# Attention on one core: in half of the row tiles GpSimd adds the row maximum and one exponential serves two tiles

## The chip, the cores and the metric

The kernel runs on one core of one Trainium2 chip. The metric is device time in microseconds (us), the median of several runs. A core has five engines with a queue each, and every queue is worked off in the order of the program: PE (TensorE, matrix products), DVE (VectorE), ACT (ScalarE), POOL (GpSimd) and SP (SyncE, which here only issues transfers). They wait for one another through semaphores. On-chip memory is SBUF (working data) and PSUM (where PE writes its results).

## What is computed

An adaptive layer norm block: attention against a given cache of keys and values, and then a mixer and an MLP. Cut to what matters here:

```python
h = _layernorm(x) * (1 + ca) + sa                       # x: 2048 rows of 640
q = (h @ wq).reshape(B, Sq, H, Dh).transpose(0, 2, 1, 3)   # 32 heads of 128
scores = einsum('bhqd,bhkd->bhqk', q, k_cache) * Dh ** -0.5   # 2048 x 2048 a head
p = softmax(scores, axis=-1)
o = einsum('bhqk,bhkd->bhqd', p, v_cache)
x = x + ga * (o.reshape(B, Sq, H * Dh) @ wo)
# then: layer norm, a shifted mixer with w1 and w2, an MLP with w3 and w4
```

Inputs and the output are bfloat16.

## The kernel before

Attention is cut into 512 *tiles* of 128 query rows against all 2048 keys: 32 heads of 16 tiles each. The loop of line 552 takes one *step* `s` for each tile (`j = s % 16` within the head), and each step appends instructions to the five queues. What a tile goes through:

1. PE: scores into `Sps` in two halves of 1024 columns (`qk`, lines 15 and 301). `Sps` holds one tile, so a half is computed anew only when DVE has read it.
2. DVE: for each half one instruction (line 594) that multiplies the scores by -1/sqrt(128), writes them as float32 into `negS` and keeps the minimum of each row (`nm0`, `nm1`). The minimum of the negated scores is minus the row's maximum. `negS` has three slots; tile `s` uses slot `s % 3`, and DVE may write it when the last reader of tile `s - 3` has finished.
3. POOL: the smaller of the two minima (line 604, `nm`).
4. ACT: the exponential (line 607), which reads `negS` with scale -1 and `nm` as its bias, and writes bfloat16 probabilities into `Pb`, a ring of ten slots (`RP`).
5. The probabilities are transposed into `PTs`, another ring of ten. For most tiles SP issues a transfer that transposes (line 231), for two tiles at once where both of a pair go that way. A few tiles (`PE_STEPS`) are transposed by PE instead, in two halves (line 262), into one of two PSUM banks (`JB`), from where ACT (line 271) or DVE (line 273) copies each half to `PTs`. `by_dve` says which halves DVE takes.
6. PE: the product with V (`pv`, line 314), `PVD` steps after the scores. V has a column of ones, so the row sums come with it.
7. ACT copies the result of two tiles to `Of` (line 585); POOL takes the reciprocal of the sums for four tiles at once (line 455), multiplies (line 462) and issues a transfer to a scratch buffer in HBM for each four tiles (line 469), `LAG` steps later.

Between these, PE computes the Q projection of the next head in pieces (line 246). It uses the same two banks as the transposes, in turn, and ACT casts each finished block of 512 rows (line 253). So PE's next user of a bank waits for the copy out of it.

Heads are of two kinds: those with `h % 4 == 1` (kind 1, eight of them) and the others (kind 0). In kind 0, PE transposes tile 3 in steps 6 and 7 and tile 10 in steps 13 and 14. In kind 1 it transposes tile 2 in steps 5 and 6, tile 3 in 7 and 8, tile 10 in 14 and 15. The pieces of Q fill the other half steps in order, so that casts come in steps 2, 4, 10 and 12 of kind 0, and in 2, 4, 11 and 13 of kind 1.

The order within a step is written out by hand. ACT gets first the copy to `Of` (every second step), then the evacuations and casts of the step, then the exponential. DVE gets the two halves and then its evacuation. POOL gets the minimum, then the reciprocal, the multiplication and the transfer, where there are any. `Prog` (line 20) keeps for each buffer key its last writer and its readers since, and from these puts a semaphore wait in front of an instruction.

After attention the output projection (line 540) and the rest follow in the same program. The first product of the output projection begins while the last tiles are still under way.

## Time and profile before

| | us |
|---|---|
| median of three runs | 1575.56 |
| the three runs | 1574.34, 1575.56, 1580.4 |
| span of the profiled execution | 1568.9 |
| PE busy in it | 1472.3 |
| DVE busy | 1398.3 |
| ACT busy | 1275.9 |
| POOL busy | 623.0 |
| first score tile on DVE starts | 35.4 |
| last exponential ends | 1255.5 |

The profiled execution's own device time is not among the three runs. The profile gives its span, from the first to the last instruction, and the median of the runs lies 6.7 us above it, which is what lies around the span.

How to read it: a line of the groups names the source line, the engine, the operation, the output and input buffers with their shapes and the number of instructions; then the busy time in us, the mean ns of one, and after the second bar the idle time of the engine just before them with what ended it. A line of the timeline begins with the start in us and the duration in us, and in square brackets there is the idle time ahead of it and what released it. An engine's shown durations overlap where one instruction starts before the one in front has quite finished; then the distance from start to start is what an instruction occupies. The granted clock is PE's, as a share of full speed.

### The profile page before, as it was taken

How to read it: one execution, taken by the hardware profiler on the slowest of the kernel's cores; microseconds unless marked ns; L12 is line 12 of the kernel's file. 1: busy time of each engine (PE TensorE's matmuls, PEld its weight loads, DVE VectorE, ACT ScalarE, POOL GpSimd, SP SyncE). 2: the span in 40 equal slices, each digit the busy share in tenths (PEclk: the TensorE clock that was granted, in tenths of full speed). 3: DMA queues.
4: the chain of work that ended last, by engine and by line, in shares of the span. 5: the costliest groups of instructions: out<-in, count | busy, mean ns of one | idle time of the engine just before them, and what ended most of it. 6: DMA issues, size and time to landing. Idle time of an engine off the chain costs nothing.

```text
span 1568.9 us, 33553 instructions
## 1 busy us (share of the span) xinstructions
PE 1472.3 (94%) x13947; PEld 923.4 (59%) x13175; DVE 1398.3 (89%) x2471; ACT 1275.9 (81%) x1121; POOL 623.0 (40%) x1396
## 2 busy tenths in 40 slices
PE   5899999999999999999999999999999899999999
PEld 3466666666665566566656666566566655554545
DVE  6999999999999999999999999999999937667435
ACT  4999999999999999999999999999999900034230
POOL 0144444444444444444444444444444433323100
PEclk9999999999999999999999999999999999999999
DMA  9999999999999999999999999999999999725100
GB/s 298 239 221 239 237 242 237 233 241 243 237 240 233 239 232 232 240 236 235 229 237 236 233 243 249 226 242 243 235 241 237 238 246 190 157 53 144 38 22 34
DMA packets 1172828, 334.59 MB, mean 213 GB/s; under 512 B 1153280, under 2 KB 1166656, under 8 KB 1172672
## 3 DMA queue, kind: packets, MB, share of 16 engines
q1 hardware_dynamic: 1164192, 311.30, 100.8%
q0 software_dynamic: 6144, 16.79, 3.5%
q10 hardware_dynamic: 2336, 4.34, 0.8%
q8 instruction: 108, 1.77, 0.5%
q14 instruction: 48, 0.39, 0.1%
HBM read 43.48 MB, written 19.40 MB: 40 GB/s over the span
## 4 chain that ended last, share of the span: by engine, by line
ACT 40%; DVE 23%; PE 19%; DMA 9%; issue 7%; POOL 1%; POOLq 0%; DVEq 0%
ACT ring L607 32%; DVE negS L594 20%; DMA ring<-ring 8%; PE Sps L540 8%; PE Sps L847 4%; ACT ring L271 3%; ACT kv L253 2%; ACT Of L585 2%; PE QPp L798 2%; PE Oaug L798 2%; DVE ring L273 1%; PE Sps L783 1%; DVE ring L379 1%; DMA negS<-o_scratch 1%; PE PTp L314 1%
## 5 line engine op out<-in xcount | busy, mean ns | idle before, releaser
L594 DVE TENSOR_SCALAR_CACHE_REDUCE negS<-Sps 128x1024 f32<-128x1024 f32 x1024 | 1177.7, 1224 | 19.4 <-PE Sps L15 18.5
L607 ACT ACTIVATE ring<-negS,small 128x2048 bf16<-128x2048 f32 x512 | 1045.7, 2066 | 13.7 <-POOL small L604 12.5
L314 PEld LDWEIGHTS PTp<-kv,ring 128*128 128x128 bf16 x8192 | 554.1, 98 | 325.0 <-issue 69.6
L314 PE MATMUL PTp<-kv,ring 128*128 128x129 bf16 x8192 | 645.3, 220 | 25.0 <-DMA ring<-ring 23.9
L15 PE MATMUL Sps<-kv 128*128 128x512 bf16 x1024 | 387.9, 379 | 16.8 <-DVE negS L594 9.9
L604 POOL TENSOR_SCALAR small<-small 128x1 f32<-128x1 f32 x512 | 146.4, 286 | 621.8 <-DVE negS L594 621.7
L301 PE MATMUL Sps<-kv 128*128 128x512 bf16 x919 | 354.3, 386 | 27.8 <-DVE negS L594 16.5
L462 POOL TENSOR_SCALAR On<-Of,small 128x128 bf16<-128x128 f32 x512 | 191.0, 373 | 13.0
L301 PEld LDWEIGHTS Sps<-kv 128*128 128x128 bf16 x1024 | 98.1, 96 | 141.7 <-DVE negS L594 121.6
L455 POOL TENSOR_TENSOR small<-Of,small 128x4 f32<-128x4 f32 x128 | 133.1, 1040 | 8.8 <-ACT Of L585 8.7
L469 POOL DMA_DIRECT2D o_scratch<-On x128 | 103.1, 806 | 40.8 <-POOL On L462 37.2
L585 ACT COPY Of<-PTp 128x259 f32<-128x259 f32 x256 | 108.6, 424 | 13.2 <-PE PTp L314 13.2
L246 PE MATMUL Oaug<-hTx,kv 128*128 128x512 bf16 x268 | 101.9, 385 | 3.7 <-DVE hTx L411 3.7
L246 PE MATMUL QPp<-hTx,kv 128*128 128x512 bf16 x259 | 97.7, 382 | 2.6 <-ACT hTx L406 2.1
L728 ACT ACT_TABLE_LOAD x1 | 1.3, 1283 | 112.6 <-POOL hTx L746 112.6
L594 DVE DVE_READ_ACCUMULATOR negS<-Sps 128x1 f32 x1024 | 90.3, 88 | 0.0
L271 ACT COPY ring<-Oaug 128x1024 bf16<-128x1024 bf16 x72 | 77.0, 1069 | 0.0
L641 POOL TENSOR_SCALAR negS<-negS 128x1 f32<-128x1 f32 x48 | 24.2, 504 | 125.2 <-DVE negS L650 125.2
L540 PE MATMUL Sps<-wo,negS 128*128 128x128 bf16 (+1 forms) x503 | 69.9, 298 | 1.2 <-DMA negS<-o_scratch 0.8
L540 PE MATMUL Sps<-wo,hTx 128*128 128x512 bf16 (+1 forms) x502 | 69.3, 297 | 0.5
L851 DVE TENSOR_TENSOR ring<-Sps,ring 128x640 f32<-128x640 f32 x15 | 12.4, 824 | 59.5 <-PE Sps L847 59.5
L655 DVE TENSOR_TENSOR ring<-Sps,mod_bc 128x640 f32<-128x640 f32 x16 | 13.1, 821 | 53.6 <-PE Sps L540 32.9
(88 smaller groups left out, 1052.7 us busy)
## 6 DMA issues: line engine op xcount, KB each, us to landing
kv<-in_A_v_cache_dram SPq DMA_DIRECT2D x32, 512.0 KB, 5.0
o_scratch<-On POOLq DMA_DIRECT2D x128, 128.0 KB, 4.7
kv<-in_A_wq_dram SPq DMA_DIRECT2D x32, 160.0 KB, 3.2
wo<-in_A_wo_dram SPq DMA_DIRECT2D x1, 5120.0 KB, 16.5
ring<-ring SPq DMA_TRANSPOSE x248, 7.1
ring<-in_A_x_dram SPq DMA_DIRECT2D x5, 640.0 KB, 6.6
ring<-in_w_mod_dram SPq DMA_DIRECT2D x1, 3200.0 KB, 13.8
out_dram<-wo SPq DMA_DIRECT2D x15, 160.0 KB, 1.8
```

Of the source, the lines that this page charges most:

```text
L15: return t.add_instruction(mybir.InstMatmult(name=t.bass.get_next_instruction_name(), ins=[t.lower_ap(rhs), t.lower_ap(lhsT)], outs=[t.low ...
L246: G.op("tensor", lambda t: t.matmul(JB[jb], wq[:, hb, q, :], hT[:, q, cc * 512:(cc + 1) * 512], start=(q == 0), stop=(q == KT - 1)), r=[(" ...
L271: G.op("scalar", lambda a: a.copy(dst, src), r=[("J", jb)], w=[("PT", g % RP, r)])
L301: ins = (t.matmul if c2 == 0 else partial(same_weights, t))(Sps[:, col:col + 512], QT[:, hb, j * 128:(j + 1) * 128], KTs[:, hb, col:col + ...
L314: ins = t.matmul(ob[:, 0:129], PTs[:, b, kt, :], Vaug[:, hb, kt, 0:129], start=(kt == 0), stop=(kt == NKT - 1))
L455: G.op("gpsimd", lambda g: g.tensor_tensor(out=rl[:, 4 * b:4 * b + 4], in0=Of[:].rearrange("p a z d -> p (a z) d")[:, 4 * b:4 * b + 4, 128 ...
L462: G.op("gpsimd", lambda g: g.tensor_scalar(out=On[:, b, z, :], in0=Of[:, 2 * b + z // 2, z % 2, 0:128], scalar1=rl[:, 4 * b + z:4 * b + z ...
L540: ins = t.matmul(YB[b][:, c0:c0 + cw], OTj[pr % 2][:, 2 * hh + z, :], wo[:, hh, c0:c0 + cw], start=(hh == 0), stop=(hh == H - 1))
L585: G.op("scalar", lambda a, p=p: a.copy(Of[:, p % 4].rearrange("p z d -> p (z d)")[:, 0:259], PO[:, (p % 2) * 512:(p % 2) * 512 + 259]), r= ...
L594: G.op("vector", lambda v, half=half, s=s, r8=r8: v.tensor_scalar(out=negS[:, s % 3, half * 1024:(half + 1) * 1024], in0=Sps[:, half * 102 ...
L604: G.op("gpsimd", lambda g, r8=r8: g.tensor_scalar(out=nm[:, r8:r8 + 1], in0=nm0[:, r8:r8 + 1], scalar1=nm1[:, r8:r8 + 1], scalar2=None, op ...
L607: G.op("scalar", lambda a, s=s, r8=r8: a.activation(Pb[:, s % RP, :], negS[:, s % 3, :], ACT.Exp, bias=nm[:, r8:r8 + 1], scale=-1.0), r=[( ...
```

## The change

In each head, the tiles 0 and 1, 4 and 5, 8 and 9, 12 and 13 become *merged pairs*. For a tile of such a pair, line 604 multiplies the minimum by -1, which gives the row's maximum. POOL then reads the tile from `negS`, adds that maximum and writes the sum as bfloat16 into the tile's slot of `Pb`. After the second tile of the pair, ACT takes one exponential over both slots, 4096 columns, in place, with scale -1 and no bias. The other eight tiles of a head stay as they were.

Two things go with it. `PVD` is 9 instead of 8, so the product with V of each tile comes one step later, and what is tied to it (the copy to `Of`, POOL's multiplication, the load of V). And `by_dve` gives DVE fewer of the copies behind PE's transposes: before, the second half of tile 3 in every head and of tile 2 in kind 1, 40 in all; after, that of tile 2 in kind 1 and that of tile 3 in every fourth head (`h % 4 == 3`), 16 in all. The 24 others go to ACT.

```diff
-                PVD = 8
+                PVD = 9
                 PE_STEPS = ({3: 6, 10: 13}, {2: 5, 3: 7, 10: 14})
                 kind = lambda h: 1 if h % 4 == 1 else 0
+                MERGED = (0, 4, 8, 12)
+                merged = lambda s: s % NQT // 2 * 2 in MERGED
...
-                by_dve = lambda g, r: r == 1 and g % NQT in (2, 3)
+                by_dve = lambda g, r: r == 1 and (g % NQT == 2 or g % NQT == 3 and g // NQT % 4 == 3)
...
-                        G.op("gpsimd", lambda g, r8=r8: g.tensor_scalar(
-                            out=nm[:, r8:r8 + 1], in0=nm0[:, r8:r8 + 1], scalar1=nm1[:, r8:r8 + 1], scalar2=None, op0=ALU.min),
+                        G.op("gpsimd", lambda g, r8=r8, sc=-1.0 if merged(s) else 1.0: g.tensor_scalar(
+                            out=nm[:, r8:r8 + 1], in0=nm0[:, r8:r8 + 1], scalar1=nm1[:, r8:r8 + 1], scalar2=sc, op0=ALU.min, op1=ALU.mult),
                             r=[("nmh", 0, r8), ("nmh", 1, r8)], w=[("nm", r8)])
-                        G.op("scalar", lambda a, s=s, r8=r8: a.activation(
-                            Pb[:, s % RP, :], negS[:, s % 3, :], ACT.Exp, bias=nm[:, r8:r8 + 1], scale=-1.0),
-                            r=[("negS", s % 3), ("nm", r8)], w=[("Pb", s % RP)])
+                        if merged(s):
+                            G.op("gpsimd", lambda g, s=s, r8=r8: g.tensor_scalar(
+                                out=Pb[:, s % RP, :], in0=negS[:, s % 3, :], scalar1=nm[:, r8:r8 + 1], scalar2=1.0,
+                                op0=ALU.add, op1=ALU.mult),
+                                r=[("negS", s % 3), ("nm", r8)], w=[("Pb", s % RP)])
+                            if s % 2 == 1:
+                                pair = ring[:, (s - 1) % RP:s % RP + 1].rearrange("p r s -> p (r s)")
+                                G.op("scalar", lambda a, pair=pair: a.activation(pair, pair, ACT.Exp, scale=-1.0),
+                                     w=[("Pb", (s - 1) % RP), ("Pb", s % RP)])
+                        else:
+                            G.op("scalar", lambda a, s=s, r8=r8: a.activation(
+                                Pb[:, s % RP, :], negS[:, s % 3, :], ACT.Exp, bias=nm[:, r8:r8 + 1], scale=-1.0),
+                                r=[("negS", s % 3), ("nm", r8)], w=[("Pb", s % RP)])
```

## The prediction

> **What bounds the kernel now.** I read the stretches of busy time first, then the groups by line, then the timeline of a few tiles in the middle of attention, which occupies 35 to 1255 us of the span. The header, a steady stretch and an early one (columns: PE, PEld, DVE, ACT and POOL busy, granted clock, DMA share, GB/s):

> ```profile
> PE 1472.3 (94%) x13947; PEld 923.4 (59%) x13175; DVE 1398.3 (89%) x2471; ACT 1275.9 (81%) x1121; POOL 623.0 (40%) x1396
> 600.00:638.00 38.00, 36.44 (x371) 23.44 (x345) 37.88 (x68) 38.00 (x33) 18.04 (x41) 1.00 1.18 231
> 52.00:56.00 4.00, 2.35 (x18) 1.30 (x16) 4.00 (x9) 3.79 (x3) 0.34 (x2) 1.00 0.25 56
> ```

> In 600 to 638 DVE and ACT are both full, PE is 96% busy and POOL has half its time free. One engine relieved alone would gain nothing. The groups give the prices:

> ```profile
> L604 POOL TENSOR_SCALAR small<-small 128x1 f32<-128x1 f32 x512 | 146.4, 286 | 621.8 <-DVE negS L594 621.7
> L462 POOL TENSOR_SCALAR On<-Of,small 128x128 bf16<-128x128 f32 x512 | 191.0, 373 | 13.0
> L273 DVE COPY ring<-QPp 128x1024 bf16<-128x1024 bf16 x40 | 27.6, 690 | 0.0
> L560 POOL TENSOR_SCALAR mod_bc<-mod_bc 128x640 f32<-128x640 f32 x1 | 0.7, 726 | 0.0
> ```

> The timeline gives the latencies, and what an ACT instruction really occupies, since its shown duration overlaps with the next one:

> ```profile
> 603.27 2.12 ACT L607 ACTIVATE ring<-negS,small 128x2048 bf16<-128x2048 f32 x1
> 605.17 1.12 ACT L271 COPY ring<-QPp 128x1024 bf16<-128x1024 bf16 x1
> 606.07 2.13 ACT L607 ACTIVATE ring<-negS,small 128x2048 bf16<-128x2048 f32 x1
> 607.97 0.49 ACT L585 COPY Of<-PTp 128x259 f32<-128x259 f32 x1
> 608.23 4.02 ACT L607 ACTIVATE ring<-negS,small 128x2048 bf16<-128x2048 f32 x2
> ...
> 613.12 1.23 DVE L594 TENSOR_SCALAR_CACHE_REDUCE negS<-Sps 128x1024 f32<-128x1024 f32 x1
> 615.60 0.28 POOL L604 TENSOR_SCALAR small<-small 128x1 f32<-128x1 f32 x1 [1.67 <-DVE negS L594]
> 616.81 2.15 ACT L607 ACTIVATE ring<-negS,small 128x2048 bf16<-128x2048 f32 x1
> 618.71 0.72 ACT L253 CAST kv<-QPp 128x512 bf16<-128x512 f32 x1
> 619.18 2.16 ACT L607 ACTIVATE ring<-negS,small 128x2048 bf16<-128x2048 f32 x1
> 619.99 1.23 DVE L594 TENSOR_SCALAR_CACHE_REDUCE negS<-Sps 128x1024 f32<-128x1024 f32 x1
> ...
> 1240.50 0.28 POOL L604 TENSOR_SCALAR small<-small 128x1 f32<-128x1 f32 x1 [1.65 <-DVE negS L594]
> 1240.82 2.00 ACT L607 ACTIVATE ring<-negS,small 128x2048 bf16<-128x2048 f32 x1 [0.27 <-POOL small L604]
> ```

> From start to start, an exponential occupies ACT 1.90 us, an evacuation L271 0.90, a Q cast 0.47, an Of copy 0.26. The tile whose first half starts on DVE at 613.12 has its minimum at 615.60 (2.48 later); its exponential ends at 618.96; at 619.99 DVE begins the tile three further on, in the same slot of negS (three slots). A half tile takes DVE 1.145 us, a tile 2.29. So **a slot is handed back about 1.0 us before it is wanted**. That margin is what this forecast turns on.

> **The change, part by part.**

> *ACT and DVE work.* A pair's exponential without bias, 128x4096: the 2048 further columns at 0.83 ns (from 0.90 less 0.47 over 512 columns) are 1.70, and the bias pointer goes. L406, with two pointers, takes 0.68 start to start (31.70 to 32.38) against 0.47 for a cast of the same width, so one is 0.10. 1.90 + 1.70 - 0.10 = 3.50 us (bounds 3.44, with a PSUM copy's small fixed cost, to 3.60) instead of 3.80. 128 pairs save ACT 38 us; 24 evacuations moved to it cost 24 x 0.90 = 22. DVE loses 24 x 0.60 (an evacuation from start to start, 58.06 to 58.66) = 14. If throughput were all, the kernel would gain 14 to 16 us.

> *GpSimd's add, 256 times.* L462 and L560 have its form: (726 - 373)/512 = 0.69 ns a column, so 373 + 1920 x 0.69 = 1.70 us. Upper bounds: at the rate of the two memsets L769 and L770 (366 ns for 320 columns, 632 for 640, so 0.83 ns) 1.97; if it took as long as DVE on a tile, 2.3. Nothing shown reads negS on POOL now, so a wait on DVE's writes could come on top; faster than 1.70 nothing shown is. I take 1.70, by the rows of its own form. [...] POOL's load, in four tiles: 2 x 1.70, 4 x 0.28, 4 x 0.37, one reciprocal 1.04, one DMA issue 0.81: 7.9 of at least 9.2 us. It fits, but in order.

> *The slots.* Tiles go in fours: a, b (merged), c, d (not). With three slots, DVE's next b must wait until the exponential of c has read its slot. That one stands in ACT's queue behind the pair (a, b), which waits for GpSimd's add of b, which waits for DVE's b. So there is a loop from the start of DVE's b to the start of DVE's next b, four tiles on:
> 2.48 (DVE b until the minimum) + 0.39 (L604 0.28, and 0.11 as between L455 and L462 on POOL, where one reads the other's result) + 1.70 (add) + 0.04 (POOL to ACT, 1240.78 to 1240.82) + 3.50 (pair) + 0.26 (Of copy of step c) + 2.05 (exponential of c to its end, with 0.05 for the signal, estimated) = **10.42 us**, where DVE's own four tiles need 9.16.
> Before, the loop is one exponential and three tiles long, and it closed with that 1.0 us to spare.

> *Evacuations inside the loop.* ACT does those of step c between the pair and exponential c. Heads of kind 0 (24): Q casts in steps 2 and 10, evacuations in 6 and 14, 2 x 0.47 + 2 x 0.90 = 2.74 a head. Kind 1 (8): 0.47 + 0.90 = 1.37. The 24 moved ones fall in steps 7 and 8 (d and a), where ACT now idles before the pair (exponential d, Of copy and two evacuations end by 4.2 us after the loop's start, the pair begins at 4.61): no cost.

> *PE's banks.* In kind 0, step 8's first Q piece reuses the bank that step 6's evacuation reads, and ACT now reaches that only after the pair: 9.4 us into the loop. Then scores of the second half (0.87 us after a Q piece starts) come at 10.3, and DVE's next b starts 0.2 late; tile a's add, norm and DMA issue on POOL (0.39 + 1.70 + 0.37 + 0.30 + 0.81 after a minimum now at 11.7) end at 15.25, 1.27 after b's minimum is ready. Together 1.47 a head. In kind 1 the same between steps 7 and 9: 0.65.

> *The rest.* PVD of 9 gives transposes a step more; the pair's lands about 16 us after the loop's start (8.1 + 7.1 median), wanted at 22. PE's 25 us of waits for them should go, but PE no longer limits. One more tile's product with V remains behind the last exponential: 1.0 us (32 matmuls took 2.04). V's load, a step later on SP, is 14 steps ahead of need. The factor -1 on L604 is free.

> *Sum.* A head of kind 0: 4 x 10.42 + 2.74 + 1.47 = 45.9; of kind 1: 41.68 + 1.37 + 0.65 = 43.7; weighted, a loop is 11.34 us. The first pair starts at 42.66 + 0.11 + 1.70 + 0.04 = 44.5, and behind it two copies L451, a cast and the exponential of tile 2 end at 51.5, when DVE begins tile 5 (before: 51.2). 126 loops later, at 1480, it begins tile 509; before, it did at 1244.9: +235. From there to the end of the last exponential it is 4.61 + 3.50 + 0.26 + 0.90 + 1.90 + 2.00 = 13.2 against 10.55: +2.6. With the 1.0: **+238.5**. On the profiled span of 1568.9 that gives 1807.4, and the median of the runs shown, 1575.56, lies 6.7 above that span: **1814 us**.

> **Rivals.**
> 1. *Not slower: the pair's exponential is quick enough for the loop to fit into DVE's four tiles.* The loop with its evacuations averages 11.0 without the bank waits, DVE's tiles 9.2 to 9.3; it decides at 1.75 us less a loop. Were ACT twice as fast on 16-bit input, the pair would take 1.80, and DVE's 14 us would be gained: 1561. Against it: L271, 16-bit in and out, costs 0.83 ns a column more than a 32-bit cast, no less. Chance 0.04.
> 2. *The add is slower than its small rows say*, by length or because DVE and POOL meet in negS. Each 0.1 us costs 126 x 0.1 and, where tile a's add is on the path, 24 x 0.1: 15 us. 1.97 to 2.6 gives 1854 to 1949. For it: only one row is longer than 128 columns, and it is alone. Chance 0.13.
> 3. *PE's clock falls* in the new gaps, up to 2.5 us in step 8. At the 0.91 of the first 40 us, eight half steps of 1.115 would take 0.88 more a loop: +111, 1925. Against it: in 52 to 56 PE was busy 2.35 of 4 us at 1.00. Chance 0.02. [...]
> 4. *The loop holds but is looser than I walk it* (bank waits hidden, signals shorter, evacuations placed elsewhere): without bank waits 1772; without the evacuations inside it too, 4 x 10.42 x 32 against 1216, about 1700. Below 1755: chance 0.07.

> **How the numbers follow.** The forecast has 0.74, with its own range 1755 to 1854. The 0.13 of rival 2 reach on from there. Leaving out about 1 in 10 on each side gives 1720 to 1890. Runs of one kernel agree to about 0.5%, which is my bound for no change. Slower: 0.74 + 0.13 + 0.02 + 0.07 = 0.96. Rival 1 gives 0.03 to faster, 0.01 to the same.

> **What would show it.** DVE's L594 should gain idle time with ACT's plain exponential as its releaser, 1 to 3 us once in four tiles, some 230 us in all; POOL's add should read 1.7 us; the pair 3.5 to 3.6; ACT should wait for POOL before each pair; PE should fall to about 82% busy at clock 1.00. I am wrong if DVE stays full, or if it waits for POOL instead of ACT.

## The result and the profile after

The changed kernel takes 1887.4 us (median; 1885.78 to 1888.02), the kernel before 1574.95 in the same comparison: the ratio is 1.1989, with a 95% interval of 1.1946 to 1.2031. That is 312 us slower. The forecast was 239 us slower (1814), with a range to 1890. Direction and mechanism came out as said; the size was some 75 us short, outside the forecast's own range (1755 to 1854) and just inside the outer one (1720 to 1890). One execution among the runs below, of 2336.21 us at a mean granted clock of 0.604, is left out of its run's median; the other three of that run had 0.978 to 0.985.

The header of the page and a stretch of 48 us in the steady part (columns as before):

```profile
span 1886.2 us, 33903 instructions
...
PE 1567.3 (83%) x14199; PEld 940.5 (50%) x13175; DVE 1401.5 (74%) x2447; ACT 1268.2 (67%) x1017; POOL 1132.0 (60%) x1652
```

```profile
700.00:748.00 48.00, 37.13 (x365) 22.84 (x332) 36.04 (x63) 37.91 (x29) 32.09 (x49) 0.96 0.88 188
```

No engine is full any more. DVE, which had 37.88 of 38 us before, has 36 of 48; ACT, which had all 38, has 38 of 48. The work of these two has hardly changed (DVE 1398 to 1402, ACT 1276 to 1268): for them the 317 us of longer span are waiting. The groups with the prices, and then the view of waits (engine, line, what it waited for: us in total, times, longest):

```profile
L596 DVE TENSOR_SCALAR_CACHE_REDUCE negS<-Sps 128x1024 f32<-128x1024 f32 x1024 | 1191.8, 1221 | 327.2 <-ACT ring L619 193.5
...
L616 ACT ACTIVATE ring<-ring 128x4096 bf16<-128x4096 bf16 x128 | 463.0, 3617 | 335.3 <-POOL ring L610 335.3
L610 POOL TENSOR_SCALAR ring<-negS,small 128x2048 bf16<-128x2048 f32 x256 | 505.9, 1976 | 23.9
```

```profile
ACT ring L616 <- POOL ring L610: 335.3, 128, 5.0
DVE negS L596 <- ACT ring L619: 193.5, 101, 3.2
...
DVE negS L596 <- PE Sps L15: 133.1, 103, 3.7
...
PE Oaug L248 <- ACT ring L273: 104.6, 39, 3.5
```

(Lines moved by two to twelve: DVE's half tile is now L596, the add L610, the pair's exponential L616, the plain one L619, the copy of a transposed half L273.) The add takes 1.976 us. ACT waits for it before each of the 128 pairs, 2.6 us on average. DVE waits for ACT's plain exponential, and for PE's scores, which are late largely because PE itself waits for ACT's copy L273.

One loop, steps 13 to 17 of a head of kind 0, in the timeline (start, duration, and in brackets the idle time ahead and what ended it):

```profile
842.06 1.22 DVE L596 TENSOR_SCALAR_CACHE_REDUCE negS<-Sps 128x1024 f32<-128x1024 f32 x1 [2.63 <-ACT ring L619]
...
844.55 0.30 POOL L606 TENSOR_SCALAR small<-small 128x1 f32<-128x1 f32 x1 [1.23 <-DVE negS L596]
...
844.94 1.98 POOL L610 TENSOR_SCALAR ring<-negS,small 128x2048 bf16<-128x2048 f32 x1
...
846.95 3.62 ACT L616 ACTIVATE ring<-ring 128x4096 bf16<-128x4096 bf16 x1 [1.46 <-POOL ring L610]
...
850.48 0.36 ACT L587 COPY Of<-PTp 128x259 f32<-128x259 f32 x1
850.73 1.01 ACT L273 COPY ring<-QPp 128x1024 bf16<-128x1024 bf16 x1
...
851.64 3.90 ACT L619 ACTIVATE ring<-negS,small 128x2048 bf16<-128x2048 f32 x2
...
853.77 1.22 DVE L596 TENSOR_SCALAR_CACHE_REDUCE negS<-Sps 128x1024 f32<-128x1024 f32 x1 [2.46 <-ACT ring L619]
```

From DVE's b to DVE's next b: 2.49 until the minimum, 0.39 until the add, 2.01 add and signal, 3.53 pair, 0.25 Of copy, 0.91 evacuation of step c, 2.13 until DVE starts = 11.71 us, where the forecast's terms for such a loop give 10.42 + 0.90 = 11.32. This is the predicted loop, link for link. The 0.39 too much are the add (0.27) and small ends (0.08 at the exponential's, 0.03 at the pair, 0.01 at the minimum).

From tile 5 (52.46) to tile 509 (1555.97) it is 126 loops of 11.93 us on average; before, 9.47; forecast, 11.34.

### The profile page after: what moved, and what is told of

Read it like the earlier page. It is cut to its first block, busy times and chain, and to the rows that moved or that the text cites. A ratio compares the mean times of both kernels' runs of the same rounds, so it can differ in the third digit from the quotient of the medians.

```text
span 1886.2 us, 33903 instructions
## 1 busy us (share of the span) xinstructions
PE 1567.3 (83%) x14199; PEld 940.5 (50%) x13175; DVE 1401.5 (74%) x2447; ACT 1268.2 (67%) x1017; POOL 1132.0 (60%) x1652
## 4 chain that ended last, share of the span: by engine, by line
ACT 35%; POOL 22%; PE 21%; DVE 16%; issue 6%; DMA 1%; POOLq 0%; DVEq 0%
ACT ring L616 21%; POOL ring L610 16%; DVE negS L596 14%; ACT ring L619 8%; PE Sps L542 7%; PE Sps L859 3%; ACT ring L273 3%; POOL small L606 3%; POOL o_scratch L471 2%; PE Oaug L810 2%; PE QPp L810 2%; ACT Of L587 2%; PE PTp L316 1%; PE Sps L303 1%; PE Sps L15 1%
## 5 line engine op out<-in xcount | busy, mean ns | idle before, releaser
L596 DVE TENSOR_SCALAR_CACHE_REDUCE negS<-Sps 128x1024 f32<-128x1024 f32 x1024 | 1191.8, 1221 | 327.2 <-ACT ring L619 193.5
L316 PEld LDWEIGHTS PTp<-kv,ring 128*128 128x128 bf16 x8192 | 578.4, 101 | 421.4 <-issue 273.2
L316 PE MATMUL PTp<-kv,ring 128*128 128x129 bf16 x8192 | 671.3, 226 | 24.1 <-ACT Of L587 20.6
L616 ACT ACTIVATE ring<-ring 128x4096 bf16<-128x4096 bf16 x128 | 463.0, 3617 | 335.3 <-POOL ring L610 335.3
L610 POOL TENSOR_SCALAR ring<-negS,small 128x2048 bf16<-128x2048 f32 x256 | 505.9, 1976 | 23.9
L619 ACT ACTIVATE ring<-negS,small 128x2048 bf16<-128x2048 f32 x256 | 504.3, 2007 | 0.0
L303 PE MATMUL Sps<-kv 128*128 128x512 bf16 x1024 | 407.2, 398 | 109.5 <-DVE negS L596 105.7
L15 PE MATMUL Sps<-kv 128*128 128x512 bf16 x1024 | 405.2, 396 | 0.0
L606 POOL TENSOR_SCALAR small<-small 128x1 f32<-128x1 f32 x512 | 151.9, 297 | 397.8 <-DVE negS L596 389.9
L248 PE MATMUL Oaug<-hTx,kv 128*128 128x512 bf16 x320 | 134.9, 426 | 108.4 <-ACT ring L273 104.6
L248 PE MATMUL QPp<-hTx,kv 128*128 128x512 bf16 x320 | 120.3, 379 | 3.3 <-ACT hTx L408 2.6
L264 PE MATMUL Oaug<-ident,ring 128*128 128x128 bf16 x576 | 56.3, 220 | 50.2 <-ACT ring L619 50.2
L248 PEld LDWEIGHTS Oaug<-hTx,kv 128*128 128x128 bf16 x320 | 34.0, 107 | 119.9 <-ACT ring L273 88.7
L596 DVE DVE_READ_ACCUMULATOR negS<-Sps 128x1 f32 x1024 | 85.1, 83 | 0.0
L273 ACT COPY ring<-Oaug 128x1024 bf16<-128x1024 bf16 x72 | 73.7, 1024 | 0.0
```

The lines of the kernel that those rows point to most:

```text
L15: return t.add_instruction(mybir.InstMatmult(name=t.bass.get_next_instruction_name(), ins=[t.lower_ap(rhs), t.lower_ap(lhsT)], outs=[t.low ...
L248: G.op("tensor", lambda t: t.matmul(JB[jb], wq[:, hb, q, :], hT[:, q, cc * 512:(cc + 1) * 512], start=(q == 0), stop=(q == KT - 1)), r=[(" ...
L303: ins = (t.matmul if c2 == 0 else partial(same_weights, t))(Sps[:, col:col + 512], QT[:, hb, j * 128:(j + 1) * 128], KTs[:, hb, col:col + ...
L316: ins = t.matmul(ob[:, 0:129], PTs[:, b, kt, :], Vaug[:, hb, kt, 0:129], start=(kt == 0), stop=(kt == NKT - 1))
L596: G.op("vector", lambda v, half=half, s=s, r8=r8: v.tensor_scalar(out=negS[:, s % 3, half * 1024:(half + 1) * 1024], in0=Sps[:, half * 102 ...
L606: G.op("gpsimd", lambda g, r8=r8, sc=-1.0 if merged(s) else 1.0: g.tensor_scalar(out=nm[:, r8:r8 + 1], in0=nm0[:, r8:r8 + 1], scalar1=nm1[ ...
```

## The experiments

Each is the changed kernel with one edit, unless it says otherwise. The kernel before took 1570.6 to 1572.5 us in the four comparisons, against 1574.95 in that of the changed kernel; gains and losses are told against the changed kernel's 1887.4, so 2 to 4 us of each gain are this difference.

### Which closing of the loop counts: a fourth slot

DVE gets four slots of `negS` instead of three. The room comes from `Pb`, eight slots instead of ten.

```diff
-                Pb = ring[:, 0:RP]
-                PTs = ring[:, RP:2 * RP].rearrange("p r (k q) -> p r k q", k=NKT)
+                PB = 8
+                Pb = ring[:, 0:PB]
+                PTs = ring[:, PB:PB + RP].rearrange("p r (k q) -> p r k q", k=NKT)
+                neg3 = flat[:, (PB + RP) * SK:2 * RP * SK].bitcast(F32)
+                nslot = lambda s: negS[:, s % 4, :] if s % 4 < 3 else neg3
...
-                                r=[("S", half)], w=[("negS", s % 3), ("nmh", half, r8)])
+                                r=[("S", half)], w=[("negS", s % 4), ("nmh", half, r8)])
```

> The changed kernel with a fourth slot in negS (it takes two of the ten slots of Pb, so Pb has eight; sizes in sum as before). Three theories. Loop: DVE's next b waits for the exponential of c in the slot three tiles back. With four slots the same chain (about 11.3 us) spans five tiles, which DVE needs 11.45 us for, so DVE should hardly wait for ACT any more. Left are PE's bank wait in step 8 of kind 0 (some 2 us in 24 heads, 50 us) and POOL's 8.9 us of work in 9.2: about 1640 us (1590 to 1700). POOL bound: POOL's work in order sets the pace; the slots matter little, 1820 to 1890. PE bound (bank waits and the lower clock behind them): also 1820 to 1890.

Measured: 1829.96 us, ratio 1.1643 (1.1622 to 1.1664). Only 57 us came back, not 247. The waits (all lines four further on):

```profile
ACT ring L620 <- POOL ring L614: 269.7, 127, 4.7
DVE negS L600 <- PE Sps L15: 266.7, 180, 4.3
...
PE Oaug L268 <- ACT ring L623: 92.7, 56, 1.8
PE PTp L320 <- ACT Of L591: 84.0, 58, 3.0
PE Oaug L252 <- ACT ring L277: 68.1, 39, 3.9
```

DVE's wait for ACT's exponential is gone, as it should be, and about every second loop (steps 1 to 5 and 9 to 13) now runs at 9.16. POOL's work is all in these loops too, so it is not POOL's total that sets the pace. But the other loops rose to between 13.0 and 14.5 us, and PE's score wait, which DVE feels, doubled to 267 us, because PE is held up by three things of ACT's: it may transpose tile 10 only after that tile's exponential, it may write the product with V only when the Of copy has emptied a bank, and it may use the bank of Q only after L277. All three stand behind the pair in ACT's queue, at about the same distance in steps as the slot. That `Pb` has two slots fewer could add to this; it was not tried by itself. **The slot is one of several closings of the loop, and taking it away alone hands the wait to PE.**

### The price of the add, on POOL's path of a and of b

A second add over the first 640 columns of the tile, from `negS` again, so that the same values are written once more; in one run for the first tile of each pair, in another for the second:

```diff
+                            if s % 2 == 0:          # second run: s % 2 == 1
+                                G.op("gpsimd", lambda g, s=s, r8=r8: g.tensor_scalar(
+                                    out=Pb[:, s % RP, 0:640], in0=negS[:, s % 3, 0:640], scalar1=nm[:, r8:r8 + 1], scalar2=1.0,
+                                    op0=ALU.add, op1=ALU.mult),
+                                    r=[("negS", s % 3), ("nm", r8), ("Pb", s % RP)], w=[("Pb", s % RP)])
```

> The changed kernel with 640 columns added once more on POOL behind the add of each tile a, the first of a pair (the same values written again): 0.8 us and a wait of 0.1. Loop: tile a's add is not in the loop. POOL has about 1.1 us free before b's minimum in the usual stretch, so it costs only where POOL is already late, in step 8 of kind 0 and a few others: 1890 to 1940. POOL bound: 128 x 0.9 = 115 us, 2000.

> The same 640 columns behind the add of each tile b, the second of a pair. Loop: this add is in the loop, so each loop is 0.9 us longer, 126 x 0.9 = 113 us: 2000 (1985 to 2030). POOL bound: the same 2000; together with the run with the extra work behind a it tells the two apart. PE bound: below 1920.

Measured: after a, 1941.65 us (ratio 1.2351, 1.2321 to 1.2381), 54 more and just above the expected range; after b, 1995.13 (1.2692, 1.2661 to 1.2722), 108 more. In the run after b, the groups read:

```profile
L621 ACT ACTIVATE ring<-ring 128x4096 bf16<-128x4096 bf16 x128 | 463.0, 3617 | 438.9 <-POOL ring L615 438.9
...
L615 POOL TENSOR_SCALAR ring<-negS,small 128x640 bf16<-128x640 f32 x128 | 102.1, 798 | 12.0
```

The short add takes 0.80 us, and behind b it delays the loop by 108/126 = 0.85 on average: **taken over all loops, add b lies on the path with its full length**. It is not so evenly spread. Steps 1 to 5 of kind 1, which have only the forecast's terms, go from 11.29 to 12.17 us; steps 5 to 9 of kind 0, where PE's bank is late as well, stay at 13.0; steps 9 to 13 rise by more. Behind a the same add costs half as much. The 798 ns also settle the rate: with 373 ns at 128 columns and 1976 at 2048 they lie on one line of 0.83 ns a column.

### The copies behind PE's transposes: all to DVE, or one more

```diff
-                by_dve = lambda g, r: r == 1 and (g % NQT == 2 or g % NQT == 3 and g // NQT % 4 == 3)
+                by_dve = lambda g, r: True
```

> The changed kernel with every copy behind a PE transpose on DVE (144 instead of 16), none on ACT. Loop: the copies in step c leave the chain between the pair and the exponential of c (0.9 us in two loops of a kind 0 head and in one of kind 1), and the bank of step 8 is free early, so PE's wait of about 2.8 us there and the lower clock behind it go: 24 x (0.9 + 0.9 + 1.5) + 8 x 1.2 = 89 us less, 1798 (1770 to 1830), and the mean clock rises from 0.96 to above 0.98. POOL bound: 1870 to 1890. If DVE were the bound it would be slower by up to 128 x 0.6 = 77.

Measured: 1872.4 us (ratio 1.1911, 1.1882 to 1.194); only 15 us came back, and the mean clock stayed at 0.962. In kind 0 the loops of steps 5 to 9 and 13 to 17, which held the copies, did fall, from 13.1 and 11.7 us to 11.0 and 11.2; but those of steps 1 to 5 and 9 to 13 rose from 11.8 and 11.9 to 12.6 and 12.5. The timeline of a loop of steps 1 to 5, in a head of kind 1, where it went from 11.3 to 12.6, shows why:

```profile
846.03 0.29 POOL L606 TENSOR_SCALAR small<-small 128x1 f32<-128x1 f32 x1 [1.66 <-DVE negS L596]
846.42 1.97 POOL L610 TENSOR_SCALAR ring<-negS,small 128x2048 bf16<-128x2048 f32 x1
...
848.36 0.37 POOL L464 TENSOR_SCALAR On<-Of,small 128x128 bf16<-128x128 f32 x1
849.03 0.80 POOL L471 DMA_DIRECT2D o_scratch<-On  x1 [0.29 <-POOL On L464]
849.88 0.31 POOL L606 TENSOR_SCALAR small<-small 128x1 f32<-128x1 f32 x1
850.28 1.98 POOL L610 TENSOR_SCALAR ring<-negS,small 128x2048 bf16<-128x2048 f32 x1
...
852.29 3.62 ACT L616 ACTIVATE ring<-ring 128x4096 bf16<-128x4096 bf16 x1 [4.47 <-POOL ring L610]
```

Tile a occupies POOL from its minimum at 846.03 to the end of the issue of the transfer at 849.83: 3.8 us. DVE brings b 2.29 us after a, so b's minimum waits 1.5 us on POOL. In the changed kernel DVE waits for its slot ahead of b, and that wait hides POOL's work for a. The time is the one expected of a bound by POOL, and in these loops it is POOL's order that counts. Take one wait away, and the other shows: the terms of the loop do not add up, the longer of two counts.

The smaller edit gives DVE only the copy that holds up the first piece of Q in step 8, where PE's longest single waits in attention are:

```diff
-                by_dve = lambda g, r: r == 1 and (g % NQT == 2 or g % NQT == 3 and g // NQT % 4 == 3)
+                by_dve = lambda g, r: r == 1 and (g % NQT == 2 or g % NQT == 3 and g // NQT % 4 == 3) or r == 0 and g % NQT == 3 and g // NQT % 4 != 1
```

> The changed kernel with one copy more a head on DVE in kind 0: the first half of tile 3 (step 6), which the bank of step 8's Q piece waits for; 24 copies move. Bank and clock theory: PE's gap of 2.8 to 3.4 us in step 8 goes, and with it the clock of 0.72 to 0.77 behind it; the loop from step 5 to 9 falls from 13.2 to about 11.2. But then DVE no longer waits ahead of step 9, and POOL's work for tile 8 (3.8 us) delays tile 9's add: the loop from 9 to 13 rises by about 1.2. In sum 24 x 0.8 = 19 us less, 1868 (1850 to 1880), mean clock above 0.98. If the gap in step 8 were a plain loss: 24 x 2 = 48 less, 1839.

Measured: 1851.22 us (ratio 1.178, 1.1745 to 1.1816), 36 less. In kind 0 the loop of steps 5 to 9 fell from 13.1 to 10.8 us, and that of steps 9 to 13 rose from 11.9 to 12.2. The clock's mean rose only from 0.962 to 0.969, not above 0.98, so that it still falls in places: from 585 to 591 us it was 0.81.

### The transfer to scratch later

What POOL does with the product with V comes two steps later: the issue of the transfer moves from step a to c and the reciprocal from b to d, away from the adds. A multiplication stays in every step. (The kernel's closing loads, which stand at fixed steps of the end, move with them.)

```diff
-                LAG = 4
+                LAG = 6
...
-                    if s == NG:
+                    if s == NG + PVD + LAG - 13:
...
-                    if s == NG + 2:
+                    if s == NG + PVD + LAG - 11:
```

> The changed kernel with LAG 6 instead of 4: on POOL the reciprocal moves from step b to d and the DMA issue from a to c, so POOL's work between a's minimum and b's falls from 3.8 to 2.7 us. If POOL in order delays b's add only where DVE has not waited ahead of b: 10 to 60 us less than 1887, 1850. If POOL's order set the pace in every loop: 128 x 1.1 = 140 less, 1750.

Measured: 1857.58 us (ratio 1.1825, 1.1777 to 1.1873), 30 less: what POOL does between a and b costs something, but by itself is no large part of the loss.

### The parts without the merging, and one pair a head

```diff
-                MERGED = (0, 4, 8, 12)
+                MERGED = ()             # second run: (0,)
```

> The changed kernel without any merged pair: PVD of 9 and the 24 copies moved from DVE to ACT are left, and line 606's second operation. ACT gains 22 us of work and was full, DVE loses 14: 10 to 22 us slower than before, about 1587 (1575 to 1600). If PVD or the copies carried part of the loss seen, more than 1620.

> The changed kernel with one merged pair a head (tiles 0 and 1) instead of four. Waits behind the pair in ACT's queue: each lone pair costs the 11.2 us of its chain less the 9.2 of DVE's four tiles, 2.0 us, once a head: 64 us over the kernel without pairs, so about 1645 (1620 to 1670). If POOL's total work were the cause (its load per head falls by 15 us) the time would be that of the kernel without pairs, 1590.

Measured: without pairs 1575.64 us, ratio 1.0036 (1.0022 to 1.005); its mean loop is 9.51 against 9.47. With one pair 1693.83, ratio 1.0786 (1.0757 to 1.0815), above the expected range. So PVD and the moved copies cost some 5 us, and the pairs all the rest. One pair costs (1693.83 - 1575.64)/32 = 3.7 us a head, while four cost (1887.4 - 1575.64)/32 = 9.7, or 2.4 each. A lone pair is dearer because its DVE arrives at full rate, so POOL's work on a delays b as above: the loops with the pair took 12.5 us on average in kind 0 and 12.1 in kind 1, those without 9.3 to 10.8.

### The order in ACT's queue: the pair behind exponential d

The pair's exponential and its transposing transfer move from behind b to behind the exponential of d. c's copies and exponential then stand ahead of it. The product with V follows one step later (PVD 10, LAG 5), since the pair's probabilities come later; the closing loads move as above. Two more things move with PVD and LAG: the Of copy, from steps a and c to b and d, and POOL's reciprocal and transfer, to d and c, as in the run with LAG 6.

```diff
-                PVD = 9
+                PVD = 10
...
-                            if s % 2 == 1:
-                                pair = ring[:, (s - 1) % RP:s % RP + 1].rearrange("p r s -> p (r s)")
-                                G.op("scalar", lambda a, pair=pair: a.activation(pair, pair, ACT.Exp, scale=-1.0),
-                                     w=[("Pb", (s - 1) % RP), ("Pb", s % RP)])
...
-                        if not is_pe(s):
+                        if not is_pe(s) and not merged(s):
...
+                        if s % 4 == 3 and merged(s - 2):
+                            m = s - 2
+                            pair = ring[:, (m - 1) % RP:m % RP + 1].rearrange("p r s -> p (r s)")
+                            G.op("scalar", lambda a, pair=pair: a.activation(pair, pair, ACT.Exp, scale=-1.0),
+                                 w=[("Pb", (m - 1) % RP), ("Pb", m % RP)])
+                            transpose(m - 1, 2)
```

> The changed kernel with the same work in another order: ACT gets the pair's exponential and SP its transposing transfer behind the exponential of d instead of ahead of step c; PVD 10 and LAG 5 so that the later transfer has time and POOL's reciprocal and DMA issue fall into steps d and c. All adds, pair exponentials and copies are still there. ACT-queue theory (what stands behind the pair, exponential c and the Of copy and copies of step c, is late for everything three steps on): these no longer wait for the add, most of the loss goes, 1610 (1580 to 1670). If the add's or the pair's own length were the cause, or POOL's total work, it stays at 1800 or above.

Measured: 1679.53 us (1676.78 to 1690.78), ratio 1.0719 (1.0652 to 1.0786), above the expected range: 208 us came back, out of 312, with the same adds, the same pairs and the same three slots. ACT's wait for the add and DVE's for the plain exponential, both shown above for the changed kernel, are gone. The pair's line in the groups, and the waits:

```profile
L626 ACT ACTIVATE ring<-ring 128x4096 bf16<-128x4096 bf16 x128 | 462.1, 3610 | 0.0
```

```profile
POOL small L606 <- DVE negS L596: 196.3, 246, 8.6
PEld PTp L316 <- issue: 139.9, 585, 0.4
PEld PTp L316 <- DMA ring<-ring: 131.5, 84, 4.0
DVE negS L596 <- PE Sps L15: 131.3, 90, 3.8
...
ACT ring L615 <- POOL small L606: 85.0, 73, 3.7
```

Two new waits are left: PE's product with V for the transposing transfer, which now starts later, and ACT's plain exponential for its minimum, which stands behind the two adds on POOL. These waits are what the expectation lacked. POOL's reciprocal and transfer stand here where LAG 6 put them, and that gave 30 by itself, so some 30 of the 208 may be due to it rather than to ACT's order; what the Of copy's move is worth was not tried by itself.

The same with two pairs a head, `MERGED = (0, 8)`, to see whether fewer of them give the rest back:

> The kernel with the pair's exponential behind that of d (PVD 10, LAG 5), but with two merged pairs a head (tiles 0 and 1, 8 and 9) instead of four. POOL has 30 us less a head to do and the pairs (4, 5) and (12, 13), whose transposes came late for PE, are gone. ACT-queue theory: near the kernel without pairs, 1575 to 1600; below 1570 only if ACT's saving (64 x 0.27 = 17 us) shows. If each pair had a fixed price wherever it stands, half of the way from 1576 to 1685: 1630.

Measured: 1752.18 us, ratio 1.114 (1.1108 to 1.1172): slower than with four pairs. The timeline:

```profile
562.33 1.98 POOL L610 TENSOR_SCALAR ring<-negS,small 128x2048 bf16<-128x2048 f32 x1
...
565.01 1.97 POOL L610 TENSOR_SCALAR ring<-negS,small 128x2048 bf16<-128x2048 f32 x1
...
567.63 2.00 ACT L615 ACTIVATE ring<-negS,small 128x2048 bf16<-128x2048 f32 x1 [2.69 <-POOL small L606]
...
571.70 3.60 ACT L626 ACTIVATE ring<-ring 128x4096 bf16<-128x4096 bf16 x1
...
575.67 2.01 ACT L615 ACTIVATE ring<-negS,small 128x2048 bf16<-128x2048 f32 x1
...
577.80 1.23 DVE L596 TENSOR_SCALAR_CACHE_REDUCE negS<-Sps 128x1024 f32<-128x1024 f32 x1 [2.24 <-ACT ring L615]
```

The pair at 571.70 is followed by the exponential of tile 4, which is a plain one here. So tile 4's slot is free only at 577.68, and DVE waits for it with tile 7. With four pairs, tile 4 belongs to a pair, and POOL's add frees its slot. The same blocking thus came back in another place. Besides, c's minimum (one small POOL instruction) stands behind the adds: DVE is done with c at 566.40, the minimum comes at 567.31, and 0.9 us of ACT's wait of 2.69 are due to that.

### The length in ACT's queue: no pair, but two exponentials

The adds stay. Each merged tile gets its own exponential in place, 2048 columns, right behind its add; that is what was merged, undone, and nothing else.

```diff
-                            if s % 2 == 1:
-                                pair = ring[:, (s - 1) % RP:s % RP + 1].rearrange("p r s -> p (r s)")
-                                G.op("scalar", lambda a, pair=pair: a.activation(pair, pair, ACT.Exp, scale=-1.0),
-                                     w=[("Pb", (s - 1) % RP), ("Pb", s % RP)])
+                            G.op("scalar", lambda a, s=s: a.activation(Pb[:, s % RP, :], Pb[:, s % RP, :], ACT.Exp, scale=-1.0),
+                                 w=[("Pb", s % RP)])
```

> The changed kernel with the pair's exponential taken apart again: each merged tile has its own exponential over its slot of Pb (2048 columns, in place, no bias, about 1.8 us), a's behind a's add, b's behind b's. GpSimd's adds and all else stay. Behind b's add then stand 1.8 instead of 3.5 us ahead of step c: the loop falls from 11.3 to 9.6 by itself; but DVE then hardly waits ahead of b, and POOL's work for a (3.8 us against 2.3 of a tile) delays b's add by about 1.1: 10.7. 128 x 0.6 to 1.7 less than 1887: about 1760 (1690 to 1810). If the length of ACT's instruction were not on the path: 1880 or, with ACT's added 35 us, more.

Measured: 1704.74 us, ratio 1.0837 (1.0816 to 1.0857): 183 us came back, and the granted clock is 0.996. The group of it and of DVE:

```profile
L596 DVE TENSOR_SCALAR_CACHE_REDUCE negS<-Sps 128x1024 f32<-128x1024 f32 x1024 | 1186.2, 1221 | 150.5 <-ACT ring L617 96.6 <-PE Sps L15 53.6 <-issue 0.2
...
L614 ACT ACTIVATE ring<-ring 128x2048 bf16<-128x2048 bf16 x256 | 493.2, 1927 | 141.2 <-POOL ring L610 141.1
```

ACT works a little more (a single one takes 1.81 us from start to start, at 766.93 to 768.74, so two take 3.62 instead of 3.53). But a's half is done while POOL still adds b, and what stands between add b and c's exponential is 1.81 instead of 3.53. That is 1.72 us a loop, 217 us in all by the loop's terms; 183 came.

### All three together

The split exponentials, LAG 6 and the one copy of tile 3 on DVE:

> The same with LAG 6 (POOL's work between the minima of a and b 2.7 us) and the first half of tile 3's copies in kind 0 on DVE. Three terms of the loop are then smaller: the pair, POOL's order, the bank of step 8. If they add up: about 9.7 us a loop, 1660 (1610 to 1710), still slower than before since GpSimd's add of 2.0 us stays between DVE and ACT.

Measured: 1630.21 us, ratio 1.0363 (1.0348 to 1.0379), with a mean loop of 9.90 us. ACT's wait for the add is down to 87 us. This is the fastest of the runs that keep GpSimd's add, and it keeps nothing of the single exponential for two tiles. The three edits gave 183, 30 and 36 us by themselves, 249 in sum, and 257 together. No version tried beats the kernel before; the nearest is the one without pairs, at 1.0036.

## Why the prediction was right, and where it was short

**The loop: right.** The forecast said that DVE's next b waits for c's exponential, which stands behind the pair, which waits for POOL's add of b. The timeline shows it link for link, a longer add b lengthens the loop by its full length on average (0.85 for 0.80), and the order and the length in ACT's queue are the cause: moved behind d, 208 us came back (some 30 of them perhaps by POOL's order); split in two with nothing else changed, 183. The loops that have only these terms fit to a few hundredths when the measured terms are put in. Steps 13 to 17 of kind 0: 11.32 + 0.39 = 11.71, measured 11.68 to 11.72 in 22 of 23 heads. Steps 1 to 5: 10.89 + 0.39 = 11.28, measured 11.28 or 11.29 in 21 of the 24 heads that do not follow one of kind 1.

**The add: its size was the step that failed.** I took 1.70 us "by the rows of its own form" and kept 1.97, the rate of the memsets, as the upper bound. It is 1.976. The slope of 0.69 ns came from two rows that differ in more than length: L462 writes bfloat16 and takes its scalar from a column, L560 writes float32 and has two constants. In the add's own form 640 columns took 798 ns in the experiment, not 726; which of the two differences makes the 72 ns was not tested. This was rival 2 at the lower end of its range. The forecast's own rule of 15 us for each 0.1 gives 41 us for the 0.276, so the add alone leads to about 1855. The rest of the way to 1887.4 is the small ends of the other links and the next two points, and it is luck that these misses, all on the slow side, still ended 3 us inside the outer range.

**The clock: rival 3, to which I gave 0.02, came in part.** I expected gaps up to 2.5 us in step 8 and a clock of 1.00. The gap there is 2.80 to 3.45 in 21 of the 22 heads of kind 0 from 2 to 30, and over the 6 us around it the granted clock was 0.72 in all 21. In head 12 the gap is 1.24 and the clock 1.00. Head 11 and head 12 in the windows, and PE's timeline in head 11:

```profile
585.92:591.92 6.00, 4.42 (x25) 2.20 (x23) 2.08 (x3) 5.58 (x6) 1.58 (x2) 0.72 0.85 194
633.51:639.51 6.00, 4.76 (x46) 2.72 (x41) 4.72 (x9) 6.00 (x6) 2.21 (x4) 1.00 0.77 176
```

```profile
587.50 0.53 PE L248 MATMUL Oaug<-hTx,kv 128*128 128x512 bf16 x1 [3.44 <-ACT ring L273]
587.82 0.63 PE L303 MATMUL Sps<-kv 128*128 128x512 bf16 x1
...
591.39 0.38 PE L248 MATMUL Oaug<-hTx,kv 128*128 128x512 bf16 x1
```

Behind the gap a product of 512 columns shows 0.63 us instead of 0.38. The loop of steps 5 to 9 takes 11.75 us in head 12 and 12.41 to 13.95 in the others from 2 to 30. That difference holds the longer gap as well as the clock, and head 12 has a half clock of its own ahead of the gap; what the clock costs was not measured by itself. The clock fell behind every gap of 2.80 us or more, and behind shorter ones in places (last section), so the 2.5 us that I expected did not rule it out. The early row that I leaned on had 1.65 us of idle time in 4, too little to show it.

**The banks: one place was missed.** In kind 1, PE's last transposes fall in steps 14 and 15, so the first piece of Q in the next head's step 0 waits for the copy of step 14, which stands behind a pair. PE waits 2.73 us there in all eight heads from 2 to 30 behind one of kind 1, and the loop of steps 1 to 5 takes 12.6 instead of 11.3. I had worked out this wait for step 8 of kind 0 and steps 7 to 9 of kind 1 only.

**The sum.** The longer terms, 0.39 in each of 126 loops, are 49 us. Steps 5 to 13 of kind 0 take 24.92 us on average; the forecast's terms for them give 23.68, and 0.39 twice is 0.78, so about 0.46 in 24 heads, 11 us, are left for the slow clock and for a gap longer than I said, less what POOL's delay of b cost less than I thought. Steps 1 to 5 behind kind 1 are 1.3 in 8 heads, 10 us. Steps 13 to 17 of kind 1 take 12.08 instead of 11.71, which is 3 us in 8 heads. These 73 us are the 74 that 126 x (11.93 - 11.34) makes. How the 11 divide was not tested by itself.

The last 6.7 us of the forecast were put in for a wrong reason. They are not all "what lies around the span": the changed kernel's execution of 1888.02 us has a span of 1886.2, so that is about 1.8, and the rest is the difference between the profiled execution of the kernel before and the median of the others. By spans the forecast is 79 us short (1807.4 against 1886.2), of which the loops are 74. Two slips are small: rival 4's 1772 should be about 1774, since 24 x 1.47 and 8 x 0.65 make 40 us, and 8.1 + 7.1 is 15.2, not "about 16".

**What I had right for an incomplete reason.** I named the slot as the place where the loop closes. It is the one that shows, but the fourth slot gave only 57 us: PE's transposes, the Of copy and the bank of Q close it at nearly the same distance.

**The rest.** The pair: 3.50 said, 3.53 from start to start, 3.6 shown. The factor -1 on the minimum, called free: 286 ns before (L604), 297 after (L606). POOL never full: 60% busy. DVE's wait for ACT: "some 230 us" said, 193.5 measured, and 133.1 for PE besides, which I had put at 1.47 a head. PE 82% busy said, 83% measured, but the one at a clock of 1.00 over 1807 us and the other at 0.962 over 1886, so that they meet is partly chance. The 38 us of ACT's work that the pairs save bought nothing: ACT was busy 81% of the span before and 67% after. PVD and the moved copies, which I put at about nothing, cost 5 us.

## What to carry to other kernels

When two instructions are merged into one on an engine that works in order, the question is not what the engine saves but what stands behind the longer instruction, and how late its last input is: here 3.5 us waiting for a 2 us add held up the slot, the banks and the transposes, and cost 307 us to save 38. Draw the loop from a buffer's reuse back to itself, add up its links with measured durations, and compare it with the engine's own time for as many tiles; when it does not fit, look for every other buffer that closes at the same distance, because freeing one alone hands the wait to the next. For a price, take rows whose input type, output type and scalars are those of the new instruction; the slope between two rows that differ in them was 17% off.

## What the runs showed of the hardware that was not expected

```profile
321.38:324.79 3.41, 1.40 (x13) 0.79 (x12) 0.92 (x3) 3.41 (x4) 0.00 (x0) 1.00 0.54 123
324.79:328.21 3.42, 3.42 (x35) 1.99 (x30) 3.10 (x7) 3.42 (x4) 2.56 (x3) 1.00 0.83 189
...
512.53:515.94 3.41, 1.31 (x12) 0.79 (x12) 0.92 (x3) 3.41 (x4) 0.04 (x1) 1.00 0.67 153
515.94:519.35 3.41, 3.41 (x18) 1.70 (x15) 2.14 (x5) 3.41 (x4) 2.45 (x3) 0.50 1.33 161
```

The gap is the same, but the grid cuts it in two places: in head 6 PE is busy for 1.40 us of the first window and the next one has the full clock, in head 10 for 1.31 us and the next one has half of it.
